# Four whole loads of keys issued as 112, 8 and 8 rows in a decode kernel of two attention layers and two gated feed-forward layers

## The chip, the cores and the metric

The kernel runs on one core of one Trainium2 chip. The metric is the device time in microseconds (us) of one execution. Before the change the median of three runs is 1331.05 us (1328.17, 1331.05 and 1331.53). The profiled execution that all lines below come from took 1329.1 us, of which 1327.3 us lie between its first and its last instruction (the span).

## The reference, cut to what matters

Two sequences (B = 2), one new token each, go through attention, feed-forward, attention and feed-forward; both attention layers read the same cache of 4096 keys and values for 16 heads of 256 numbers, all in float32.

```python
def _A_ref(x, k_cache, v_cache, wq, wo):
    q = (x @ wq).reshape(B, Sq, H, Dh).transpose(0, 2, 1, 3)
    scores = jnp.einsum("bhqd,bhkd->bhqk", q, k_cache) * (Dh ** -0.5)
    p = softmax(scores, axis=-1)
    o = jnp.einsum("bhqk,bhkd->bhqd", p, v_cache)
    return o.transpose(0, 2, 1, 3).reshape(B, Sq, H * Dh) @ wo
def _B_ref(x, W_gate, W_up, W_down):
    gate = x @ W_gate; up = x @ W_up
    return (gate * (gate > 0) * up) @ W_down
x = x + _A_ref(_layernorm(x), A_k_cache, A_v_cache, A_wq, A_wo)
x = x + _B_ref(_layernorm(x), B_W_gate, B_W_up, B_W_down)
x = x + _A_ref(_layernorm(x), A_k_cache, A_v_cache, A_wq, A_wo)
x = x + _B_ref(_layernorm(x), B_W_gate, B_W_up, B_W_down)
```

One layer's keys and values are 2 x 16 x 4096 x 256 numbers each, 268 MB together. They don't fit on the core, so nearly all of them are read twice, once for each attention layer.

## The kernel before, in words

Work goes by *units*. A unit is one head of one sequence, `(h, b)`; there are 32. The first attention pass takes them in the order `first` = (0,0), (0,1), (1,0), ..., (15,1), and the second in the opposite order, so that what the first pass read last can stay on the core for the second. Each unit has 4 MB of keys and 4 MB of values. On the host the keys are laid out so that each of the 128 rows of a unit's keys is one contiguous run of 8192 numbers (32 KB); the same holds for the values. Row p goes to partition p of the core's memory.

The memory for loads is one tile, `arena`: 6 blocks of four slots and 3 single slots, a slot being 8 KB on each partition (1 MB). The class `Arena` hands slots out. A *whole load* (`n == NC`, that is 4) takes a block and brings a unit's 4 MB of keys or of values with one DMA; loads of one slot are used at the ends of the passes, for the head weights (`w_head`, 7 KB a row) and for the feed-forward weights (`w_in`, `w_out`).

`pending` is the list of all loads in the order in which they're to be issued: for each unit its keys, for every second unit the next head's weights, then its values; at the end of a pass the feed-forward weights. `pump` (lines 112 to 134) goes down this list. It takes slots for the first load; if there are none, it stops. If there are, it issues the load on SyncE's queue (SP) at line 132 and goes on. `pump` is called at the start and by `release`, which the compute steps call after the last instruction that reads a slot. So SP's instructions stand in one fixed order: each load waits for the instructions that last read its slots, then it's issued. The loads in flight are as many as the arena has room for.

A load of 128 rows is shared by the core's 16 DMA engines, eight rows each. Only the very last load of the program is cut today: its last 448 columns come as a DMA of their own, in two of 120 and 8 rows (the slices in line 131).

Compute of a unit: `score` (line 332) multiplies the keys by the query on TensorE, one slot at a time, `score_copy` and `score_turn` bring the scores into rows, `softmax_max` and `softmax_exp` use GpSimd and ScalarE, `weigh` (line 392) multiplies by the values, and `project` adds to the output `y`. The order of the instructions on each engine is the program's order (`manual_schedule`); `score` reads columns of a block over all 128 partitions, so it can start when all rows of that unit's load have landed.

In the second pass 22 of the slots hold what the first pass left (`KEPT`), so that the stretch between the passes has few free slots, and the loads there are small.

Of the kernel before, what the change touches and what calls it, by code (L numbers as in the profile page):

```python
# [15 lines left out]
P = 128  # L16
# [5 lines left out]
NC = NT // CT  # L22
# [5 lines left out]
SMALL = 13  # L28
ENDS = 4
AHEAD = 4  # L30
EPS = 1e-5
SCALE = DH**-0.5

# [32 lines left out]
def two_layers(  # L66
# [10 lines left out]
    nc = tc.nc  # L77
# [19 lines left out]
    def source(key, n):  # L97
        kind, name, c = key
        if kind in "kv":
            h, b = name  # L100
            if kind == "k":
                rows = k_cache[b, h]
            else:
                rows = v_cache[b, h].rearrange("(p t) d -> p (t d)", t=NT)
            return rows[:, c * UNIT : (c + n) * UNIT]
        if kind == "h":
            return w_head[name]
        if kind == "in":
            return w_in[c]
        return w_out[:, (14 * c + 2) // 4 * D : (14 * c + 16) // 4 * D]  # L110

    def pump():
        while pending:
            at = None
            for i, ((kind, name, c), n) in enumerate(pending[: AHEAD if pending[0][1] == 1 else 1]):
                if i and kind != "h":
                    continue
                last = at_of.get((kind, name, c - 1)) if kind in "kv" else None
                at = units.take(n, kind, last)
                if at is not None:  # L120
                    break
            if at is None:
                return
            pending.pop(i)
            src = source((kind, name, c), n)
            dst = arena[:, at * UNIT : at * UNIT + src.shape[1]]
            parts = [0, src.shape[1]]
            if not pending:
                parts[1:1] = [src.shape[1] - D]
            for i, j in zip(parts, parts[1:]):  # L130
                for p in (slice(0, 120), slice(120, P)) if i else (slice(0, P),):
                    nc.sync.dma_start(dst[p, i:j], src[p, i:j])
            for k in range(n):
                at_of[kind, name, c + k] = at + k

# [4 lines left out]
    def release(*key):  # L140
        units.free.add(at_of.pop(key))
        pump()
# [42 lines left out]
    found_s = consts.tile([P, 2 * DH], F32, name="found_s")  # L185
    nc.scalar.dma_start(row[:B, :D], x.rearrange("b s d -> (b s) d"))
    pump()


# [19 lines left out]
    eps_t = consts.tile([P, 1], F32, name="eps_t")  # L209
    nc.vector.memset(eps_t, EPS)  # L210

# [434 lines left out]
```

## Time and profile before

| | |
|---|---|
| median of three runs | 1331.05 us |
| profiled execution | 1329.1 us |
| its span | 1327.3 us, 13785 instructions |
| TensorE matmul busy | 953.9 us (72%) |
| VectorE, ScalarE, GpSimd busy | 134.7, 92.1 and 47.7 us |
| read from HBM | 561.52 MB, 423 GB/s over the span |
| whole loads of keys, of values | 59 and 58, of 4096 KB each |

How to read the lines of the profile: PE is TensorE's matmuls and PEld its weight loads, DVE is VectorE, ACT ScalarE, POOL GpSimd, SP SyncE; SPq is SyncE's sequencer, which issues the loads. L132 is line 132 of the kernel before. In a line of a group of instructions stand its line, engine, operation, the tile written and the tiles read and the count, then the busy time in us and the mean length of one in ns, then the idle time of the engine just before them and what ended it. In the table by stretches of time each row holds the stretch, its length, the busy time and the count of each engine, TensorE's granted clock (1.00 is full), the mean busy share of the 16 DMA engines, and the GB/s that they moved; the share may come out a little over 1.00 since a packet's time overlaps the next one's. The "DMA queue" lines give packets, MB and the time of the packets as a share of 16 engines over the whole span; q8 and q14 are the core's own fetches of instructions.

### The profile page before, as it was taken

To read this page: it belongs to the slowest core of one execution; us is meant where nothing else is said; L and a number is where in the kernel's file an instruction comes from. 1 tells how busy PE (TensorE), PEld (TensorE's weight loads), DVE (VectorE), ACT (ScalarE), POOL (GpSimd) and SP (SyncE) were. 2 spreads that over 40 slices of the span, in tenths; PEclk is the share of its full clock that TensorE was granted. 3 is DMA by queue.
4 is the path that set the end of the run, shared out by engine and by line. 5 is a ranking of instruction groups with operands and counts; after the bars stand their busy time and mean duration, and the time that the engine had idled before them with its cause. 6 is when DMAs were issued, how large, how long until landed. Compare 5 with 4: busy or idle time off the path is not lost.

```text
span 1327.3 us, 13785 instructions
## 1 busy us (share of the span) xinstructions
PE 953.9 (72%) x6076; PEld 321.5 (24%) x6076; DVE 134.7 (10%) x457; ACT 92.1 (7%) x280; POOL 47.7 (4%) x134
## 2 busy tenths in 40 slices
PE   4758777866677676687788967666776676766777
PEld 2223123221222221222243322222122121222213
DVE  1100011010110110000101111011011010101100
ACT  1000000000000000000011000000000000000001
POOL 0000000000000000000000000000000000000000
PEclk9786776677777876766798887787778777777779
DMA  9999999999999999999999999999999999999997
GB/s 403 434 427 430 430 427 436 428 433 426 427 436 432 429 430 426 433 433 428 422 370 403 430 430 430 431 430 430 430 429 431 431 432 427 430 434 430 430 422 300
DMA packets 27871, 562.42 MB, mean 424 GB/s; under 512 B 3101, under 2 KB 3235, under 8 KB 10019
## 3 DMA queue, kind: packets, MB, share of 16 engines
q1 hardware_dynamic: 27803, 561.53, 99.0%
q8 instruction: 48, 0.79, 0.2%
q14 instruction: 12, 0.10, 0.0%
q10 hardware_dynamic: 8, 0.01, 0.0%
HBM read 561.52 MB, written 0.00 MB: 423 GB/s over the span
## 4 chain that ended last, share of the span: by engine, by line
PE 61%; another core or an unknown queue 20%; DMA 12%; DVE 3%; issue 2%; ACT 1%; POOL 0%; SPq 0%; POOLq 0%; ACTq 0%; DVEq 0%
PE pob L392 12%; PE rawa L332 12%; PE rawb L332 12%; PE poa L392 11%; PE small L346 5%; PE pq L308 4%; DMA arena<-in_k_cache_dram 4%; DMA arena<-in_v_cache_dram 3%; DMA arena<-in_w_in_dram 3%; PE small L418 3%; DVE found_s L340 3%; DMA arena<-in_w_out_dram 2%; PE pq L311 1%; PE y L248 1%
## 5 line engine op out<-in xcount | busy, mean ns | idle before, releaser
L332 PE MATMUL rawb<-arena,q_pad 128*2 128x512 f32 x1024 | 177.3, 828 | 96.3 <-DMA arena<-in_k_cache_dram 96.3
L332 PE MATMUL rawa<-arena,q_pad 128*2 128x512 f32 x1024 | 176.9, 825 | 92.2 <-DMA arena<-in_k_cache_dram 91.7
L392 PE MATMUL poa<-arena,probs 128*2 128x512 f32 x1024 | 167.7, 815 | 72.7 <-DMA arena<-in_v_cache_dram 46.3
L392 PE MATMUL pob<-arena,probs 128*2 128x512 f32 x960 | 176.6, 902 | 47.0 <-DMA arena<-in_v_cache_dram 47.0
L346 PE MATMUL small<-ident,found_s 128*128 128x8 f32 x512 | 73.3, 270 | 35.5 <-DVE found_s L340 35.4
L346 PEld LDWEIGHTS small<-ident,found_s 128*128 128x128 f32 x512 | 67.4, 205 | 97.9 <-DVE found_s L340 97.9
L392 PEld LDWEIGHTS poa<-arena,probs 128*2 128x2 f32 x1024 | 30.3, 104 | 182.5 <-issue 137.3
L332 PEld LDWEIGHTS rawb<-arena,q_pad 128*2 128x2 f32 x1024 | 24.0, 95 | 191.0 <-DMA arena<-in_k_cache_dram 120.8
L332 PEld LDWEIGHTS rawa<-arena,q_pad 128*2 128x2 f32 x1024 | 24.2, 94 | 187.7 <-issue 172.2
L392 PEld LDWEIGHTS pob<-arena,probs 128*2 128x2 f32 x960 | 29.1, 110 | 166.1 <-issue 166.0
L360 ACT ACTIVATE nm<-top,nsr 128x1 f32<-128x1 f32 x64 | 18.8, 294 | 713.7 <-POOL top L355 713.7
L418 PEld LDWEIGHTS small<-ones,row 128*128 128x128 f32 x256 | 45.7, 253 | 89.9 <-issue 79.1
L355 POOL PARTITION_ALL_REDUCE top<-mx x64 | 22.5, 352 | 1164.7 <-DVE mx L353 1151.3
L308 PE MATMUL pq<-xs,arena 128*128 128x2 f32 x384 | 61.0, 275 | 0.5 <-DVE xs L264 0.5
L308 PEld LDWEIGHTS pq<-xs,arena 128*128 128x128 f32 x384 | 57.6, 225 | 2.0 <-issue 1.3
L418 PE MATMUL small<-ones,row 128*128 128x1 f32 x256 | 51.2, 304 | 2.6 <-DVE row L410 2.2
L427 DVE COPY oT<-small 128x2 f32<-128x2 f32 x64 | 10.2, 159 | 353.0 <-PE small L418 353.0
L410 DVE SCALAR_TENSOR_TENSOR row<-pob,ri,row 128x256 f32<-128x256 f32 x30 | 14.5, 483 | 218.5 <-ACT row L405 218.5
L410 DVE SCALAR_TENSOR_TENSOR row<-poa,ri,row 128x256 f32<-128x256 f32 x32 | 15.5, 483 | 179.6 <-ACT row L405 179.6
L405 ACT ACTIVATE row<-pob,ri 128x256 f32<-128x256 f32 x32 | 15.2, 474 | 254.6 <-PE pob L392 241.6
L340 DVE COPY found_s<-rawb 128x512 f32<-128x512 f32 x32 | 22.1, 691 | 87.5 <-PE rawb L332 87.5
L340 DVE COPY found_s<-rawa 128x512 f32<-128x512 f32 x32 | 22.1, 692 | 76.8 <-PE rawa L332 76.8
(79 smaller groups left out, 310.6 us busy)
## 6 DMA issues: line engine op xcount, KB each, us to landing
arena<-in_k_cache_dram SPq DMA_DIRECT2D x59, 4096.0 KB, 54.9
arena<-in_v_cache_dram SPq DMA_DIRECT2D x58, 4096.0 KB, 55.3
arena<-in_w_head_dram SPq DMA_DIRECT2D x31, 896.0 KB, 54.1
arena<-in_v_cache_dram SPq DMA_DIRECT2D x14, 1024.0 KB, 10.5
arena<-in_w_in_dram SPq DMA_DIRECT2D x14, 896.0 KB, 26.2
arena<-in_k_cache_dram SPq DMA_DIRECT2D x8, 1024.0 KB, 13.2
arena<-in_w_out_dram SPq DMA_DIRECT2D x4, 896.0 KB, 17.4
arena<-in_w_out_dram SPq DMA_DIRECT2D x3, 672.0 KB, 11.9
```

Of the source, the lines that this page charges most:

```text
L248: nc.tensor.matmul(y[at : at + B, : w_h.shape[1]], stat, w_h, **flags)
L308: nc.tensor.matmul(pq[:, j, :], w[:, at : at + P], xT[:, c, :], start=(c == 0), stop=False)
L311: nc.tensor.matmul(pq[:, j, :], w[:, FULL * DH : FULL * DH + P], xT[:, FULL + j, :], start=False, stop=True,)
L332: nc.tensor.matmul(raw[u % 2][32 * g : 32 * g + 2, :], q_of[u][:, j, 1 - half : 3 - half], kt[:, g, :], start=(c == 0), stop=(c == NC - 1),)
L340: nc.vector.tensor_copy(found_s, raw[u % 2])
L346: nc.tensor.matmul(s[:, :, e, :], found_s[:, e * P : (e + 1) * P], pick, start=True, stop=True,)
L355: nc.gpsimd.partition_all_reduce(mx_of[u], mx, P, RED.max)
L360: nc.scalar.activation(nm, mx_of.pop(u), AF.Copy, scale=nsr[:, b : b + 1])
L392: nc.tensor.matmul(po_of[u][32 * t : 32 * t + 2, :], p_of[u][:, n : n + 2], vt[:, 2 * t * DH : (2 * t + 2) * DH], start=(c == 0), stop=(c ...
L405: nc.scalar.activation(row[:, :DH], po_of[u][:, :DH], AF.Copy, scale=r_of[u][:, 0:1])
L410: nc.vector.scalar_tensor_tensor(row[:, :DH], po_of.pop(u)[:, DH:], r_of[u][:, 1:2], row[:, :DH], op0=ALU.mult, op1=ALU.add,)
L418: nc.tensor.matmul(pT_of[u][:, c : c + 1], row[:, c * P : (c + 1) * P], ones, start=True, stop=True,)
```

## The change

A new constant names two units. Where `pump` issues a whole load of keys of one of them, it now issues three DMAs in place of one: rows 0 to 111, rows 112 to 119, and rows 120 to 127. The values of these units, and all other loads, stay as they are. Each unit is loaded once in each pass, so there are four such loads: in the first pass the units at places 10 and 20 of 32, in the second those at places 11 and 21. The bytes, the slots and the order of the loads are the same. A DMA of 112 rows gives each of the 16 engines seven rows; a DMA of eight rows goes to eight engines, one row each. Line 131's cut of the program's last load is dropped by the same edit: `rows` is (0, 128) for it, so that its last 448 columns come as one DMA of 128 rows.

```diff
 AHEAD = 4
+UNEVEN = ((5, 0), (10, 0))
 EPS = 1e-5
@@ in pump()
             for i, j in zip(parts, parts[1:]):
-                for p in (slice(0, 120), slice(120, P)) if i else (slice(0, P),):
-                    nc.sync.dma_start(dst[p, i:j], src[p, i:j])
+                rows = (0, 112, 120, P) if n == NC and name in UNEVEN and kind == "k" else (0, P)
+                for p, r in zip(rows, rows[1:]):
+                    nc.sync.dma_start(dst[p:r, i:j], src[p:r, i:j])
             for k in range(n):
                 at_of[kind, name, c + k] = at + k
```

## The prediction

> **What bounds the kernel now.** I read the page first: the DMA rows, then the groups of TensorE.
>
> ```profile
> span 1327.3 us, 13785 instructions
> DMA  9999999999999999999999999999999999999997
> q1 hardware_dynamic: 27803, 561.53, 99.0%
> q8 instruction: 48, 0.79, 0.2%
> L332 PE MATMUL rawb<-arena,q_pad 128*2 128x512 f32 x1024 | 177.3, 828 | 96.3 <-DMA arena<-in_k_cache_dram 96.3
> L332 PE MATMUL rawa<-arena,q_pad 128*2 128x512 f32 x1024 | 176.9, 825 | 92.2 <-DMA arena<-in_k_cache_dram 91.7
> arena<-in_k_cache_dram SPq DMA_DIRECT2D x59, 4096.0 KB, 54.9
> arena<-in_w_out_dram SPq DMA_DIRECT2D x1, 210.0 KB, 14.6
> ```
>
> SP's queue has the DMA engines at work for 99.0% of the span, and TensorE's idle time before the scores ends with a load of keys. So the loads bound the kernel, and a load is issued 54.9 us before it lands: many are queued on each DMA engine. Next, the stretches: a steady one, then the ends of both passes cut fine.
>
> ```profile
> core 0: us, PE busy (x) PEld busy (x) DVE busy (x) ACT busy (x) POOL busy (x), PEclk, DMA share, GB/s
> 30.00:640.00 610.00, 442.58 (x2640) 148.11 (x2640) 59.90 (x196) 37.13 (x120) 22.06 (x60) 0.72 1.00 430
> ...
> 666.00:668.00 2.00, 2.00 (x22) 0.71 (x20) 0.00 (x0) 0.23 (x1) 0.00 (x0) 1.00 0.97 401
> 668.00:670.00 2.00, 1.57 (x15) 0.88 (x15) 0.16 (x1) 0.41 (x2) 0.00 (x0) 1.00 0.74 308
> 670.00:672.00 2.00, 1.73 (x15) 1.19 (x17) 0.33 (x2) 0.31 (x2) 0.00 (x0) 1.00 0.49 195
> 672.00:674.00 2.00, 2.00 (x24) 0.67 (x24) 0.18 (x2) 0.00 (x0) 0.00 (x0) 1.00 0.36 57
> ```
>
> ```profile
> 1314.00:1315.00 1.00, 0.80 (x9) 0.26 (x10) 0.00 (x0) 0.00 (x0) 0.00 (x0) 1.00 0.98 396
> 1315.00:1316.00 1.00, 0.57 (x6) 0.10 (x2) 0.62 (x1) 0.00 (x0) 0.00 (x0) 1.00 0.89 330
> 1316.00:1317.00 1.00, 1.00 (x11) 0.96 (x12) 0.00 (x0) 0.00 (x0) 0.00 (x0) 1.00 0.66 231
> 1317.00:1318.00 1.00, 1.00 (x19) 0.60 (x18) 0.18 (x1) 0.00 (x0) 0.00 (x0) 1.00 0.54 220
> 1318.00:1319.00 1.00, 1.00 (x18) 0.52 (x13) 0.00 (x0) 0.00 (x0) 0.00 (x0) 1.00 0.50 203
> 1319.00:1320.00 1.00, 1.00 (x8) 0.26 (x3) 0.00 (x0) 0.00 (x0) 0.00 (x0) 1.00 0.49 190
> 1320.00:1321.00 1.00, 0.37 (x9) 0.17 (x12) 0.00 (x0) 0.00 (x0) 0.00 (x0) 1.00 0.21 57
> 1321.00:1322.00 1.00, 0.80 (x16) 0.27 (x8) 0.00 (x0) 0.07 (x1) 0.00 (x0) 1.00 0.05 20
> ```
>
> In the steady stretch all 16 engines are busy and move 430 GB/s, 26.9 each. At the end the share doesn't fall at once: it drops to about a half by 1317, stays at 0.50 and 0.49 until 1320, and then goes to nothing. Half of the engines run dry early. With x the share, the late half works (4 x 0.5 + 0.49 + 0.21 + 0.05) / 0.5 = 5.5 us past 1315, the early half the other 0.39 + 0.16 + 0.04, over 0.5, or 1.2 us: **4.3 us** apart. At the end of the first pass the same stair stands at 0.74, 0.49 and 0.36. The instruction queue q8 offers a reason: 0.2% of 16 engines over 1327.3 us is 42 us (32 to 53 with the rounding), 21 in each pass; on half of the engines it is 2.7 us each. Which engines these are, no row says.
>
> **The change part by part.**
>
> *The rows moved.* A whole load is 4096 KB, or 4.194 MB; at 430 GB/s it takes 9.75 us, and one 32 KB row takes its engine an eighth, 1.22 us. Nine rows in place of eight cost the first eight engines 1.22 us in each such load; seven save the others as much. Two loads a pass make plus and minus 2.44 us, 4.88 us between the halves, about the 4.3 us read above. If each row costs what it costs now, and the late half is just the last eight, a pass ends up to 2.44 us earlier.
>
> *How the rows travel.* The trace before has no 32 KB rows in a DMA of eight rows. Its only narrow pieces, 120 and 8 rows of the last load, are the very end of the table. The bounds: at least 1.22 us for such a DMA (each engine writes its row at its usual speed), at most 9.75 us (the eight go one behind another, like the eight rows of one engine today). The nearest row is 1320 to 1321, when little but the last pieces is left: 0.21 of 16 engines is 3.4 busy engines, and they move 57 GB/s, 17.0 each and not 26.9. The second before, with wider loads in it, has 190 / (0.49 x 16) = 24.2. Busy engines that move 0.63 of their usual bytes look like engines that wait for one another at the place they write to. I take those 57 GB/s as what a narrow piece gets: 8 x 32,768 B / 57 GB/s = **4.6 us**, between the bounds. It's the weakest step here, since these rows were only 1792 B long and short rows alone could cost speed.
>
> [...]
>
> *The sum for one such load on the first eight engines*: seven rows at 1.22 are 8.5 us, two narrow pieces 9.2, together 17.7 in place of 9.75, so **+8.0 us**. What follows on these engines is queued behind, and as the engines are busy all the time, nothing is caught up within the pass: +16.0 us for two. The piece of 112 rows may itself lie between 8.5 us and the full load's 9.75, as its seven rows an engine no longer fall on the same places as eight; I take half, 0.6 a load, 1.2 a pass. That makes 17.2.
>
> *What of it shows.* The first eight engines may end a pass early today; between 0 us (they're as late as the others) and 4.3 of it is hidden. As no row tells which half is which, I take 3, nearer the upper end, since only a half that is all of one kind gives so clean a stair: 17.2 - 3 = 14.2 us a pass. Each pass's end follows its slowest engine: the last product waits for the last piece of `w_out`, and the stretch before 674 has the engines idle until the first pass's compute frees slots.
>
> ```profile
> 1303.31 17.41 DMA arena<-in_w_out_dram
> 1320.76 0.53 PEld L248 LDWEIGHTS y<-arena,near 128*2 128x2 f32 x16 [1.13 <-DMA arena<-in_w_out_dram]
> L132 SPq DMA_DIRECT2D arena<-in_k_cache_dram x67: 327/328/811, 1.2 to 1224.2; - x67
> ```
>
> *SP.* Eight DMAs more, 328 ns each, 2.6 us in all. They're hidden by the 54.9 us for which loads are queued ahead; without that cover they'd cost the 2.6. Behind the three issues of a load only the next loads wait. The wait for a slot isn't new, but TensorE now waits for three landings and not one, the last of which is late by the sum above; it then has 54.9 us of work queued less some 17 of lag, so the engines that are ahead don't run dry. Lost cover there would show as a share under 1.00 inside a pass.
>
> *The last load.* It comes as 128 rows again: eight engines lose one 1792 B row and the sixteenth engine gets eight. At 26.9 GB/s that is 0.07 and 0.53 us; if the sixteenth is among the early ones it's nothing, if it's the last, 0.5 later; one narrow piece less may give 0.2 back. I take 0.
>
> *The sum*: 1329.1 + 2 x 14.2 = 1357.5 us for the profiled execution. The median of the runs shown is 1331.05, 1.95 higher, so **1359.5 us** for the median of after.
>
> **The rivals.**
>
> *The balance works* (faster). Narrow pieces run at 1.22 us and the late half is the last eight: the late engines end 2.44 us earlier, the early ones later by 2.44 and just meet them. 1331.05 - 2 x 2.44 = 1326.2. For it: the stair's 4.3 us against the 4.88 of the change. Against: the 57 GB/s, and that the late engines needn't be the last eight.
>
> *The wrong engines* (no gain, though pieces run at full speed). If the late ones stand on both sides, some of the first eight are late and get 2.44 more a pass, at most 4.9 in all; where they're a little less late than the latest it's about 1. 1331 to 1336, I say 1332. The trace doesn't speak against it.
>
> *Full speed nearly* (a little slower). Each engine of a narrow piece keeps the 17.0 GB/s that it had at 1320, since their rows don't all collide: 32,768 / 17.0 is 1.93 us a piece. A load costs 8.5 + 3.9 - 9.75 = 2.7, a pass 5.4 - 3 = 2.4: 1335.9.
>
> *The neighbours join in* (much slower). The other engines go on with the next load and write the last rows too, so that ten rows and not eight share the 57 GB/s: 5.7 us a piece, a load 8.5 + 11.5 - 9.75 = 10.2, a pass 20.5 + 1.2 - 3 = 18.7: 1368.4. With lag growing through the second load it could reach 25 a pass, 1381.
>
> *The cut isn't what it says.* If a DMA of eight rows isn't spread over eight engines but goes through one, a piece takes 9.75 us on that one engine: 8.5 + 19.5 - 9.75 = 18.3 a load, 36.5 - 3 a pass: 1398. The program's last load, cut in that way, landed 14.6 us after its issue among others that did so too, which speaks against a special path but doesn't tell how many engines took part.
>
> [...]
>
> **How the numbers follow.** Forecast 0.38, neighbours 0.19, one engine 0.03, nearly full speed 0.10, wrong engines 0.18, balance 0.12. Predicted is 1359.5. A measurement of this kernel can tell about 0.3%, 4 us, from no change. Faster by more: the balance, 0.12, of which 0.02 stays inside: 0.10. Within: those 0.02, most of the wrong engines (0.17) and 0.05 of the nearly full speed: 0.24. Slower: 0.66. For 8 in 10 the range leaves out the balance's 0.10, the serial case and the far end of the neighbours: 1329 to 1384. The forecast's own range, with narrow pieces between 3.5 and 5.7 us and 0 to 4.3 hidden, is 1346 to 1374.
>
> **What would show it.** If I'm right, the whole loads of keys that are cut land later, TensorE's idle time before line 332 grows by some 8 us at four places, the share stays near 1.00 until the pass's end, and then the stair at about half is three or four times as long as now. The narrow pieces, 256 KB each, stand in the list of issues. If the balance works, the stair is gone: the share falls from 0.9 to nothing within two us, and the span is 4 to 5 us shorter. If the stair is as long as now with the same span, the wrong engines were relieved. I'm wrong at the first step if the DMA share falls inside a pass, and at the narrow pieces if the time is below 1340.

## The result and the profile after

The change makes the kernel **slower by 5.7%**: 1405.09 us (1403.47 to 1407.99) against 1330.22 us for the kernel before, ratio 1.0572 with a 95% interval of 1.056 to 1.0585. That is 74.9 us, or 18.7 us for each of the four loads that are cut. The direction was forecast, the size was not: 1359.5 us were predicted, and 1405 lies above the range. The profiled execution took 1403.47 us.

The page of the profile after, in the order of the lines shown of before (the edit moves the later lines down by two, so that 332 is now 334; the row of GB/s is the span in 40 equal slices):

```profile
span 1401.7 us, 13801 instructions
DMA  9999999999999999999989999999999999999996
GB/s 399 440 430 431 430 429 238 429 430 429 431 426 274 365 429 430 432 429 429 420 334 411 430 429 430 368 316 430 429 430 433 419 213 429 434 431 432 429 422 252
q1 hardware_dynamic: 27860, 561.53, 98.6%
L334 PE MATMUL rawb<-arena,q_pad 128*2 128x512 f32 x1024 | 197.1, 911 | 133.3 <-DMA arena<-in_k_cache_dram 133.3
L334 PE MATMUL rawa<-arena,q_pad 128*2 128x512 f32 x1024 | 171.2, 801 | 126.7 <-DMA arena<-in_k_cache_dram 125.0
arena<-in_k_cache_dram SPq DMA_DIRECT2D x4, 3584.0 KB, 70.4
```

The DMA engines are as busy as before and the bytes are the same; what fell is what busy engines move. Four dips stand in the row of GB/s, each at one of the cut loads: 238, 274 with 365, 368 with 316, and 213. TensorE's idle time before the scores that ends with a load of keys grew from 188.0 to 258.3 us, 70.3 of the 74.9. That is no exact account, since TensorE's waits for values fell from 93.3 to 79.9 us, and its busy time grew from 953.9 to 972.7 us at a mean granted clock of 0.735 in place of 0.762; the bytes that the engines moved, further down, are the firmer count. Where the wait for keys falls is shown by the longest single waits (us in total, times, longest), before (L332) and after (L334):

```profile
PE rawb L332 <- DMA arena<-in_k_cache_dram: 96.3, 27, 4.5
PE rawa L332 <- DMA arena<-in_k_cache_dram: 91.7, 28, 4.6
PE rawb L334 <- DMA arena<-in_k_cache_dram: 133.3, 27, 19.7
PE rawa L334 <- DMA arena<-in_k_cache_dram: 125.0, 26, 19.3
```

Cut finer around the first of these loads, after the kernel's own columns of stretches (engines' busy time, granted clock, DMA share, GB/s):

```profile
190.00:210.00 20.00, 14.99 (x72) 3.55 (x72) 1.33 (x3) 0.47 (x1) 0.00 (x0) 0.59 1.04 433
210.00:226.00 16.00, 10.64 (x54) 5.39 (x53) 1.14 (x5) 1.24 (x4) 0.73 (x2) 0.61 1.00 234
226.00:238.00 12.00, 0.00 (x0) 0.00 (x0) 0.00 (x0) 0.00 (x0) 0.00 (x0) 0.50 0.96 131
238.00:258.00 20.00, 12.83 (x84) 3.52 (x84) 1.92 (x6) 1.24 (x4) 0.73 (x2) 0.76 0.98 415
```

Two steps. For 16 us the engines move 234 GB/s, which is 3.74 MB, about the piece of 112 rows (3.67 MB). Then come 12 us at 131 GB/s, and the two narrow pieces must lie there: TensorE has nothing left to do, as it waits for them. Against 430 GB/s the first step loses 16 x (1 - 234/430) = 7.3 us, the second 12 x (1 - 131/430) = 8.3 us.

Which engines are slow can be read from the trace's own records of packets, most of which are one row of 32 KB. From 206 to 245 us 15 to 17 of them are in flight at every moment, so all 16 engines are at work throughout. (The DMA share counts a packet where it starts; that is why a short stretch can show 0.96 or 1.04.) Before 208 us a row takes 1.22 us in the median. Rows that start from 212 to 224 take 1.75 to 2.60 us, and rows that start from 228 to 234.5 take 4.08 to 4.74 us. None is fast. How a DMA's rows are shared shows in the packets too. They stand in 16 series at a time, in each of which a row starts a few ns from another's end, and I read a series as one engine. In the profile before, eight rows of a whole load come between two packets of 4 B (707 times from 100 to 600 us, where series can be followed). In this first cut load it's seven, and then a packet of 4 B stands behind each single row of the narrow pieces: 32 such packets start from 222 to 239, and 16 + 8 + 8 are 32. In five series two such single rows stand one behind the other. The counts of packets under 512 B say the same of the experiments below: four more DMAs of 64 rows are 64 more packets (`r64`, 3165 against 3101), 16 more of eight rows are 128 (`r96_c8`, 3229). In this first load 30 rows took over 4.0 us, and the two pieces have only 16 rows: the engines without a narrow piece are as slow as those with one.

The same reckoning over the four dips, after one row of before for comparison:

```profile
200.00:260.00 60.00, 48.91 (x260) 18.98 (x264) 5.41 (x19) 3.24 (x11) 2.20 (x6) 0.61 1.01 434
```

```profile
200.00:260.00 60.00, 33.32 (x184) 11.69 (x188) 3.91 (x13) 2.48 (x8) 1.47 (x4) 0.61 1.01 319
400.00:480.00 80.00, 42.27 (x260) 12.63 (x260) 5.77 (x19) 3.24 (x11) 2.20 (x6) 0.68 1.00 330
890.00:960.00 70.00, 39.38 (x236) 12.62 (x240) 5.79 (x19) 3.45 (x12) 2.20 (x6) 0.71 1.01 343
1110.00:1170.00 60.00, 28.21 (x144) 10.62 (x144) 3.31 (x10) 2.00 (x7) 1.47 (x4) 0.62 1.00 298
```

The losses are 15.5, 18.6, 14.2 and 18.4 us, 66.7 in all, so nine tenths of the change's cost lie in these four stretches. In this profile the second cut load of each pass costs more than the first.

The end of the program:

```profile
1382.00:1384.00 2.00, 1.94 (x24) 0.47 (x16) 0.00 (x0) 1.63 (x2) 0.00 (x0) 1.00 1.02 409
1384.00:1386.00 2.00, 1.64 (x17) 0.54 (x13) 0.49 (x3) 0.46 (x2) 0.00 (x0) 1.00 0.89 366
1386.00:1388.00 2.00, 1.22 (x14) 0.33 (x10) 0.00 (x0) 0.00 (x0) 0.00 (x0) 1.00 0.59 237
1388.00:1390.00 2.00, 1.57 (x15) 0.65 (x7) 0.62 (x1) 0.00 (x0) 0.00 (x0) 1.00 0.21 84
1390.00:1391.00 1.00, 1.00 (x13) 0.68 (x16) 0.19 (x1) 0.00 (x0) 0.00 (x0) 0.75 0.12 50
...
1392.00:1393.00 1.00, 1.00 (x7) 0.26 (x2) 0.00 (x0) 0.00 (x0) 0.00 (x0) 0.50 0.13 54
...
1394.00:1395.00 1.00, 1.00 (x20) 0.40 (x15) 0.00 (x0) 0.00 (x0) 0.00 (x0) 1.00 0.05 18
```

The stair at one half, which stood from 1317 to 1320 before, is gone. The share falls to 0.21 by 1388, and then a tail goes on to 1396 in which about two of the 16 engines work (0.12 x 16). By the same reckoning the stretch from 1384 to 1396 loses 8.3 us, where the end before, from 1314 to 1322, lost 4.2; the end of the first pass loses 1.0 us more than before. So half of the engines did not carry the extra time to the end of the pass, as the prediction had it: 66.7 us are lost by all 16 where the cut loads are, and some 5 us more where a few engines end a pass late.

### The profile page after: what moved, and what is told of

It reads as the page before. It is cut to its first block, busy times and chain, and to the rows that moved or that the text cites. A ratio compares the mean times of both kernels' runs of the same rounds, so it can differ in the third digit from the quotient of the medians.

```text
span 1401.7 us, 13801 instructions
## 1 busy us (share of the span) xinstructions
PE 972.7 (69%) x6076; PEld 327.9 (23%) x6076; DVE 134.8 (10%) x457; ACT 92.1 (7%) x280; POOL 47.7 (3%) x134
## 3 DMA queue, kind: packets, MB, share of 16 engines
q1 hardware_dynamic: 27860, 561.53, 98.6%
## 4 chain that ended last, share of the span: by engine, by line
PE 59%; another core or an unknown queue 22%; DMA 12%; DVE 3%; issue 2%; ACT 1%; POOL 0%; SPq 0%; POOLq 0%; ACTq 0%; DVEq 0%
PE rawb L334 12%; PE rawa L334 11%; PE poa L394 11%; PE pob L394 10%; DMA arena<-in_k_cache_dram 7%; PE small L348 5%; DMA arena<-in_v_cache_dram 3%; PE pq L310 3%; PE small L420 3%; DVE found_s L342 2%; DMA arena<-in_w_in_dram 2%; PE pq L313 1%; PE y L250 1%; DMA arena<-in_w_out_dram 0%
## 5 line engine op out<-in xcount | busy, mean ns | idle before, releaser
L334 PE MATMUL rawb<-arena,q_pad 128*2 128x512 f32 x1024 | 197.1, 911 | 133.3 <-DMA arena<-in_k_cache_dram 133.3
L334 PE MATMUL rawa<-arena,q_pad 128*2 128x512 f32 x1024 | 171.2, 801 | 126.7 <-DMA arena<-in_k_cache_dram 125.0
L394 PE MATMUL poa<-arena,probs 128*2 128x512 f32 x1024 | 174.1, 843 | 73.3 <-DMA arena<-in_v_cache_dram 49.9
L394 PE MATMUL pob<-arena,probs 128*2 128x512 f32 x960 | 169.0, 868 | 30.0 <-DMA arena<-in_v_cache_dram 30.0
L334 PEld LDWEIGHTS rawb<-arena,q_pad 128*2 128x2 f32 x1024 | 25.1, 99 | 239.2 <-DMA arena<-in_k_cache_dram 139.5
L394 PEld LDWEIGHTS poa<-arena,probs 128*2 128x2 f32 x1024 | 31.5, 106 | 188.0 <-issue 140.3
L334 PEld LDWEIGHTS rawa<-arena,q_pad 128*2 128x2 f32 x1024 | 24.4, 94 | 217.6 <-issue 202.6
L412 DVE SCALAR_TENSOR_TENSOR row<-poa,ri,row 128x256 f32<-128x256 f32 x32 | 15.5, 484 | 186.6 <-ACT row L407 186.6
```

Source lines behind the costliest of these rows:

```text
L334: nc.tensor.matmul(raw[u % 2][32 * g : 32 * g + 2, :], q_of[u][:, j, 1 - half : 3 - half], kt[:, g, :], start=(c == 0), stop=(c == NC - 1),)
L394: nc.tensor.matmul(po_of[u][32 * t : 32 * t + 2, :], p_of[u][:, n : n + 2], vt[:, 2 * t * DH : (2 * t + 2) * DH], start=(c == 0), stop=(c ...
L412: nc.vector.scalar_tensor_tensor(row[:, :DH], po_of.pop(u)[:, DH:], r_of[u][:, 1:2], row[:, :DH], op0=ALU.mult, op1=ALU.add,)
```

## The experiments

All kernels below are the kernel before, with one or more whole loads of keys cut in another way; the cut of the program's last load stays as it was (but in `ctl_cut`). The common edit, and then only its third line, which says which rows and columns each DMA takes:

```diff
+UNEVEN = ((5, 0), (10, 0))
+    def cuts_of(n, kind, name, i, j):
+        if n == NC and name in UNEVEN and kind == "k":
+            return [(p, 0, NC * UNIT) for p in (...)]
+        rows = (slice(0, 120), slice(120, P)) if i else (slice(0, P),)
+        return [(p, i, j) for p in rows]
-                for p in (slice(0, 120), slice(120, P)) if i else (slice(0, P),):
-                    nc.sync.dma_start(dst[p, i:j], src[p, i:j])
+                for p, a, b in cuts_of(n, kind, name, i, j):
+                    nc.sync.dma_start(dst[p, a:b], src[p, a:b])
```

My theory after the result: the rows of a short piece go to few places of the memory, and the engines that write there share what the places take (A). The rivals: each DMA more has its price (B), or the unequal shares themselves cost the time (C).

**Number of DMAs: `cols3`.**

```diff
+            return [(slice(0, P), a, b) for a, b in ((0, 7168), (7168, 7680), (7680, 8192))]
```

> The four whole loads of keys come as three DMAs each, as in the change, but cut by columns: 128 rows with 7168, 512 and 512 of the 8192 columns. Theory A (the places in memory that the rows of a short piece go to limit it): no change against before, 1330 us within 0.3%, since every DMA still goes to all 128 rows. Rival B (each further DMA, its issue and its landing cost the time): eight more DMAs as in the change, so the change's 75 us, 1405 us. Rival C (nine rows on one half of the engines and seven on the other): no change, each engine has eight rows.

Measured: 1329.41 against 1328.74 us, ratio 1.001 (1.0001 to 1.0019). Eight DMAs more, cut by columns, cost at most 0.2%. B falls.

**Halves: `r64`.**

```diff
+            return [(p, 0, NC * UNIT) for p in (slice(0, 64), slice(64, 128))]
```

> The four whole loads of keys come as two DMAs each, rows 0 to 63 and rows 64 to 127, every engine four rows of each. [...] Rival B (number of DMAs): one more DMA a load and not two, half of the change's 75 us, 1367 us; the run with cuts by columns tells it from A. Rival C (unequal engines): no change, 1330 us.

Measured: 1382.75 us, ratio 1.0407 (1.0391 to 1.0422), +54.0 us or 13.5 a load. All engines have equal shares here, and it still costs nearly three quarters of the change. C falls as the main cause. The stretch of the slow load, in `r64`:

```profile
190.00:210.00 20.00, 14.14 (x82) 4.26 (x82) 1.92 (x6) 0.70 (x3) 0.43 (x2) 0.74 1.02 428
210.00:232.00 22.00, 6.64 (x45) 2.17 (x44) 1.04 (x4) 1.24 (x4) 0.69 (x2) 0.69 1.01 203
```

About half of the speed, 203 of 430 GB/s, but for longer than one load: 13.5 us are lost and not the 9.75 of a load at half speed. The packets show that all engines are alike here too: every row of 32 KB that starts from 212 to 226 takes 2.33 to 2.72 us, against 1.22. In the four dips 139 to 174 rows take over 1.5 us, where the load has 128, so rows of the neighbouring loads are slow as well; that adds to the 9.75.

**Equal shares with the change's first piece: `r112_16`.**

```diff
+            return [(p, 0, NC * UNIT) for p in (slice(0, 112), slice(112, 128))]
```

> The four whole loads of keys come as 112 and 16 rows, so that every one of the 16 engines carries seven rows and one: the change's first piece, without its unequal shares. Theory A (places): the piece of 112 rows moves 238 GB/s as in the profile of after, 15.4 us for 3.67 MB and not 8.5, and 16 neighbouring rows are as slow as eight and eight were, 115 GB/s, 4.6 us and not 1.2: +10.3 us a load, +41 us, 1371 us. Rival C (unequal engines): no change, 1330 us. Rival B: one more DMA a load, 1367 us.

Measured: 1384.73 us, ratio 1.0418 (1.04 to 1.0435), +14.0 us a load where A said 10.3. Without any unequal share, three quarters of the change's price are there. The first of these loads in `r112_16`:

```profile
210.00:222.00 12.00, 10.57 (x54) 5.40 (x53) 1.13 (x5) 1.24 (x4) 0.73 (x2) 0.60 0.98 242
222.00:234.00 12.00, 0.00 (x0) 0.00 (x0) 0.00 (x0) 0.00 (x0) 0.00 (x0) 0.54 0.99 178
```

So 112 rows are as slow here, at 242 GB/s, as in the change, with no piece of eight rows behind them.

**The rest of the edit: `ctl_cut`.**

```diff
-        rows = (slice(0, 120), slice(120, P)) if i else (slice(0, P),)
+            return [(slice(0, P), i, j)]
+        rows = (slice(0, P),) if i else (slice(0, P),)
```

> Only the other part of the edit: the program's last 448 columns come as one DMA of 128 rows in place of 120 and 8. All theories: no change, 1330 us within 2 us, as the prediction took 0 for it; if the cut was worth something, up to 1 us longer.

Measured: 1328.58 us, ratio 0.9997 (0.9988 to 1.0006). The cut of the last 448 columns is worth nothing that can be measured.

**Bytes or a fixed price: `eighth`.**

```diff
+            return [(slice(0, P), 0, 7168)] + [(p, 7168, 8192) for p in (slice(0, 112), slice(112, 120), slice(120, P))]
```

> The four loads come as 128 rows for 7168 of the 8192 columns, and the cut into 112, 8 and 8 rows is made in the last 1024 columns only. Theory A (bandwidth of the places): the loss goes by the bytes in the short pieces, an eighth of 75 us, +9 us, 1339 us. Rival B' (a fixed price of a short or unequal DMA, whatever its bytes): the change's 75 us, 1404 us.

Measured: 1338.93 against 1329.46 us, ratio 1.007 (1.0054 to 1.0087): +9.5 us, where an eighth of 74.9 is 9.4. The price goes by the bytes that are cut into 112, 8 and 8 rows. Rows of 4 KB cost the same per byte here as rows of 32 KB.

**Where the rows go: `r96_c8` and `r96_s8`.** Same engines, bytes and number of DMAs; only the rows of the four pieces differ.

```diff
+            return [(p, 0, NC * UNIT) for p in (slice(0, 96), slice(96, 104), slice(104, 112), slice(112, 120), slice(120, 128))]
```

> One of a matched pair. The four whole loads of keys come as rows 0 to 95 (six rows an engine) and then four DMAs of eight neighbouring rows, 96 to 103, 104 to 111, 112 to 119, 120 to 127. Theory A (places): 96 rows at the 2.2 us a row of the change's first piece are 13.2 us, four narrow pieces at 4.6 us are 18.4, together 31.6 us in place of 9.75: +22 us a load, +87 us, 1416 us. Rival C (unequal engines: ten rows on eight engines, six on the others): 2 rows more, 2.4 us a load, at most +10 us, and the same as its twin.

```diff
+            return [(p, 0, NC * UNIT) for p in (slice(0, 96), slice(96, 128, 4), slice(97, 128, 4), slice(98, 128, 4), slice(99, 128, 4))]
```

> The twin: the same DMAs on the same engines with the same bytes, but each of the four DMAs of eight rows takes every fourth row, 96, 100, ..., 124, then 97, 101, ..., 125, and so on. [...] Rival C (unequal engines): the same as its twin. Rival D (a DMA of eight rows is slow wherever its rows go): the same as its twin.

Measured: 1437.8 us with neighbouring rows, ratio 1.0821 (1.0797 to 1.0846), and 1409.42 us with every fourth row, 1.0596 (1.0578 to 1.0613). The twins differ by 28.4 us, 7.1 a load: C and D fall as stated, since both say the same for both. But the neighbouring pieces are dearer than A's sum of 1416 us, and the spread ones aren't cheap either: which rows are taken makes 28.4 of the 108.3 us that the neighbouring pieces cost; the spread ones still cost 80.0. The stretches of the neighbouring pieces, in `r96_c8`:

```profile
210.00:224.00 14.00, 8.10 (x53) 3.17 (x52) 1.23 (x5) 1.24 (x4) 0.73 (x2) 0.71 1.03 224
224.00:244.00 20.00, 0.00 (x0) 0.00 (x0) 0.00 (x0) 0.00 (x0) 0.00 (x0) 0.50 1.00 134
```

and of the strided ones, in `r96_s8`:

```profile
210.00:224.00 14.00, 5.97 (x32) 1.00 (x32) 0.48 (x1) 0.47 (x1) 0.00 (x0) 0.62 1.02 225
224.00:238.00 14.00, 0.00 (x0) 0.00 (x0) 0.00 (x0) 0.00 (x0) 0.00 (x0) 0.50 0.99 201
```

The 96 rows run at 224 and 225 GB/s in both. The pieces then take all 16 engines to 134 GB/s where rows are neighbours and to 201, about half of 430, where they're spread. In both the DMA share stays at 1.00 and 0.99: the eight engines without a piece are busy and slow too. The packets say the same: rows that start from 229 to 236 take 2.45 to 2.55 us in `r96_s8`, those from 229 to 240 take 3.78 to 4.24 us in `r96_c8`, and none takes 1.22.

**Every second row: `r64s2`.**

```diff
+            return [(p, 0, NC * UNIT) for p in (slice(0, 128, 2), slice(1, 128, 2))]
```

> [...]

The two DMAs of 64 rows of `r64`, but the even and the odd rows in place of the halves. Measured: 1329.43 against 1328.96 us, ratio 1.0007 (0.9997 to 1.0017): no price at all, where the same two DMAs with the halves cost 54 us. The stretch in which `r64` had 203 GB/s, here:

```profile
210.00:232.00 22.00, 16.73 (x110) 8.01 (x114) 2.57 (x10) 2.00 (x7) 1.47 (x4) 0.73 1.01 434
```

So two DMAs of 64 rows aren't slow as such: neighbours run at 203 GB/s, every second row at 434. But neighbouring rows alone aren't it either: 128 of them run at 430 GB/s, and 112, seven eighths, at 234. One statement could cover both, engines that meet at one place share it and a DMA's shape decides whether they meet; it is argued, not shown: no run tells which rows share a place. Nor do these runs tell the writing from the reading: each cut changes the rows that are read from HBM together with the partitions that are written, so a cause on the reading side stands untested.

**The pieces on the other side: `r96_e8` and `r96_ec8`.** First rows 32 to 127, then pieces in rows 0 to 31, every fourth row in the one and neighbours in the other.

```diff
+            return [(p, 0, NC * UNIT) for p in (slice(32, 128), slice(0, 32, 4), slice(1, 32, 4), slice(2, 32, 4), slice(3, 32, 4))]
```

> As the run with 96 rows and four strided pieces of eight, mirrored: first rows 32 to 127, then rows 0, 4, ..., 28, then 1, 5, ..., 29, and so on. [...] Rival D' (a strided or narrow piece costs what it cost in the run before, 1409 us, wherever it goes): 1409 us.

```diff
+            return [(p, 0, NC * UNIT) for p in (slice(32, 128), slice(0, 8), slice(8, 16), slice(16, 24), slice(24, 32))]
```

> As the run with rows 32 to 127 first and strided pieces in rows 0 to 31, but the four pieces are neighbouring rows: 0 to 7, 8 to 15, 16 to 23, 24 to 31. [...] If a blocked engine also holds up engines that write elsewhere, all 16 fall to one speed and the total is about the 128 GB/s of the run with neighbouring pieces in rows 96 to 127. [...]

Measured: `r96_e8` 1384.65 us, ratio 1.043 (1.0407 to 1.0452), 24.8 us shorter than the strided pieces in rows 96 to 127, so D' falls. `r96_ec8` 1410.68 us, ratio 1.0619 (1.0599 to 1.0638), 26.0 us longer than `r96_e8`. The stretches of `r96_e8`:

```profile
210.00:224.00 14.00, 9.55 (x51) 4.87 (x51) 1.14 (x5) 1.23 (x4) 0.73 (x2) 0.68 1.03 226
224.00:229.00 5.00, 0.00 (x0) 0.00 (x0) 0.00 (x0) 0.00 (x0) 0.00 (x0) 0.68 0.92 236
229.00:249.00 20.00, 13.39 (x72) 3.73 (x76) 1.43 (x5) 0.76 (x3) 0.73 (x2) 0.59 1.00 429
```

and of `r96_ec8`:

```profile
224.00:242.00 18.00, 0.00 (x0) 0.00 (x0) 0.00 (x0) 0.00 (x0) 0.00 (x0) 0.55 0.97 180
```

Spread over rows 0 to 31, the pieces are through 5 us after the 96 rows; spread over rows 96 to 127, it took 14. So the place matters, and not the stride by itself. With neighbours in rows 0 to 31 the total is 180 GB/s, and not the 134 of `r96_c8`. The packets again show no engine at full speed: no row of 32 KB that starts from 225 to 239 takes less than 2.34 us, where an undisturbed one takes 1.22. So the slowness reaches engines without a piece here too, at a higher common speed than I had; how, these runs don't say.

**One unit at a time: `one` and `other`.**

```diff
+UNEVEN = ((5, 0),)
```

> The change for one of the two units only, (5, 0), once in each pass. Theory A: each such load costs the same by itself, so half of the change's 75 us: 1367 us. If the first such load of a pass is partly hidden by the early engines, as the prediction had it, the saving is uneven: less than half is left, below 1362.

```diff
+UNEVEN = ((10, 0),)
```

> The change for the other unit only, (10, 0), once in each pass. The change costs 75 us and (5, 0) alone 33. If each load costs by itself and the two units differ: 75 - 33 = 42 us, 1371 us. If a pass hides part of one load but not of a second one: the same 33 us as with (5, 0) alone, 1362 us.

Measured: 1362.06 us, ratio 1.0245 (1.0218 to 1.0272), and 1365.83 us, 1.0281 (1.0247 to 1.0314): +32.6 and +36.9 us, with intervals of 29 to 36 and 33 to 42 us, which overlap. The first lies at the border of its two cases, the second between its two values, so neither decides. Together they make 69.5, a little less than the change's 74.9, but the 5.4 us of difference lie within the intervals. That the second load of a pass costs more, by 3 to 4 us, stands only in the four dips of the one profile read above; its cause is open.

**The balance without blocks of rows: `clean10_6` against `r32s4`.** Every second row across all 128 is free (ratio 1.0007), and so is every fourth (1.0009, the control below), so a load can be cut without the 112 rows. The control keeps eight rows on each engine:

```diff
+UNEVEN = ((10, 0),)
+            return [(p, 0, NC * UNIT) for p in (slice(0, 128, 2), slice(1, 128, 4), slice(3, 128, 4))]
```

> Control for the run with ten and six rows: the whole load of keys of unit (10, 0), once in each pass, comes as rows 0, 2, 4, ... (64 rows), then 1, 5, 9, ... and 3, 7, 11, ... (32 rows each), every engine eight rows in all. If every second row was free because each engine still kept to its own places, every fourth row is free too: no change, 1329 us within 2 us. If 32 rows meet as 64 neighbouring ones did (+13.5 us a load for the whole of it), half of each such load is slow: +13 us, 1342 us.

```diff
+UNEVEN = ((10, 0),)
+            return [(p, 0, NC * UNIT) for p in (slice(0, 128, 2), slice(1, 128, 4), slice(3, 32, 4), slice(35, 64, 4), slice(67, 96, 4), slice(99, 128, 4))]
```

> What the change was to do, with pieces that meet as little as can be: the same load of (10, 0), once in each pass; of the control's last 32 rows each eight go in a DMA of their own: 3, 7, ..., 31, then 35, ..., 63, then 67, ..., 95, then 99, ..., 127. The first eight engines carry ten rows and the others six: in one load what the change moves in two. Balance theory (engines set the end of a pass, and the late half is the last eight): up to 2.4 us a pass shorter than the control, 4.9 us in all, 1324 us, if the pieces are free. [...]

Measured, beside 1328.15 us of before: the control 1329.27 us, ratio 1.0009 (1.0 to 1.0017); ten and six rows 1341.35 us, 1.0095 (1.0081 to 1.0109). The version with unequal shares is 12.1 us slower than its control, 6.0 a load. What they do to the end of the program stands in these two tables, the control first:

```profile
1319.00:1320.00 1.00, 0.64 (x6) 0.67 (x6) 0.21 (x1) 0.00 (x0) 0.00 (x0) 1.00 0.70 235
1320.00:1321.00 1.00, 1.00 (x16) 0.67 (x19) 0.19 (x1) 0.00 (x0) 0.00 (x0) 1.00 0.61 244
1321.00:1322.00 1.00, 1.00 (x24) 0.56 (x14) 0.00 (x0) 0.00 (x0) 0.00 (x0) 1.00 0.52 208
1322.00:1323.00 1.00, 1.00 (x12) 0.43 (x7) 0.00 (x0) 0.00 (x0) 0.00 (x0) 1.00 0.45 181
1323.00:1324.00 1.00, 0.53 (x7) 0.03 (x8) 0.00 (x0) 0.00 (x0) 0.00 (x0) 1.00 0.40 134
```

and with ten and six rows:

```profile
424.00:434.00 10.00, 0.90 (x12) 0.00 (x0) 0.48 (x1) 0.47 (x1) 0.00 (x0) 0.66 1.03 262
...
1325.00:1326.00 1.00, 0.21 (x5) 0.16 (x8) 0.00 (x0) 0.00 (x0) 0.00 (x0) 1.00 0.90 375
1326.00:1327.00 1.00, 1.00 (x10) 0.17 (x2) 0.15 (x1) 0.00 (x0) 0.00 (x0) 1.00 0.85 326
1327.00:1328.00 1.00, 0.57 (x5) 0.41 (x4) 0.47 (x1) 0.00 (x0) 0.00 (x0) 1.00 0.78 314
1328.00:1329.00 1.00, 1.00 (x9) 0.72 (x9) 0.19 (x1) 0.00 (x0) 0.00 (x0) 0.68 0.56 176
1329.00:1330.00 1.00, 1.00 (x15) 0.56 (x15) 0.00 (x0) 0.00 (x0) 0.00 (x0) 0.50 0.31 115
1330.00:1331.00 1.00, 1.00 (x11) 0.29 (x3) 0.00 (x0) 0.00 (x0) 0.00 (x0) 0.50 0.14 52
```

The stair near a half turns into one near 0.9, from which the share falls to 0.14; then it stays at 0.12 and 0.13 to 1333, which is about two engines. Most engines now end nearly together, but the end as a whole isn't more even, by one profile of each: against 430 GB/s it loses 6.8 us from 1323 to 1335, where the control loses 4.8 from 1318 to 1326. The pieces cost more than that: 10 us at 262 GB/s in the first such load and 10 us at 253 in the second lose 8.0 us together. What evening out would be worth if the pieces were free stays open: no cut was found that gives unequal shares at full speed.

## Why the prediction was wrong, step by step

*What bounds the kernel*: right. SP's queue still has the DMA engines at work for 98.6% of the span, and nine tenths of the loss are bytes that these busy engines didn't move while the cut loads came in.

*The narrow pieces*: the size was close. Taken were 4.6 us for a piece and 9.2 us for the two of a load; the rows in that stretch take 4.08 to 4.74 us each, and the stretch lasts 12 us. That is luck in part, since the 57 GB/s behind it came from rows of 1792 B at the very end, with 3.4 engines busy. That it matters which rows a piece takes was shown by the twins (28.4 us), and that the price goes by the bytes by the cut in an eighth of the columns (9.5 us). The mechanism, engines that wait for one another at the place they write to, covers a part at most: engines without a piece are as slow, and whether writing is what they wait for is open.

*The piece of 112 rows*: **this step failed**. It was taken as at most as slow as a full load, 8.5 to 9.75 us with 0.6 of loss; that its rows fall on other places than those of a full load was my estimate, and no run shows where rows fall. The stretch has 234 GB/s for 16 us, a loss of 7.3 us a load, and `r112_16` has 242 GB/s. The upper bound was no bound: I let a DMA of fewer rows cost no more than one of 128, as if 16 engines with seven rows each wrote as freely as with eight. `r64` shows that equal shares on 16 engines can run at half speed, 203 GB/s. Why seven neighbouring rows an engine are slow and eight aren't stays open.

*What of it shows*: **failed too**. The prediction charged the first eight engines alone and let 3 us a pass disappear in their being early. All 16 engines slow down, with 16 packets in flight and 131 GB/s, and the stair at a half was gone at the end and not three or four times as long. No hidden part shows: the ends of the two passes lose some 5 us more than before, and not less. This is the rival of the neighbours, and it went further than its 1381: that rival let only the two rows of the usual writers join.

The sum, measured in place of forecast: 7.3 + 8.3 is 15.6 us for the first cut load where 8.0 + 0.6, less the hidden 1.5, was forecast; the second loads add about 3 to 4 us each in this profile, and the ends of the passes some 5 us in all.

*SP*: right. Cut by columns, as many DMAs cost 0.2% at most. *The last load*: right, ratio 0.9997. *The balance*: its chance of 0.12 was for pieces at full speed, which there were none of; `clean10_6` shows that unequal shares take away the stair at a half, but leave about two engines late, so that the end loses more and not less.

The signs named in advance came out mixed: TensorE's idle time grew by 17.6 us and not by 8 at four places, the share stayed near 1.00, and the stair did the opposite of what was said: it went, and a tail of about two engines came in its place.

No version here beats the kernel before.

## What to carry to other kernels

Don't split a load by blocks of rows to shift work between DMA engines without measuring it: in this kernel blocks of 112, 96 and 64 neighbouring rows ran at 234, 225 and 203 GB/s, about half of the 430 of 128 rows, with equal shares too (`r112_16` 242, `r64` 203). If a load has to be cut, try columns first, or every second or fourth row across all 128: each was free here (ratios 1.001, 1.0007 and 1.0009), while every fourth row within a block of 32 was not (201 GB/s in rows 96 to 127, 236 in rows 0 to 31). And when a DMA share stays at 1.00 while the GB/s fall, as to 234 and 131 here, look first at which rows each DMA takes, not at how many DMAs or bytes there are.

## What the runs showed of the hardware

Unexpected were three things. Loads of 112, 96 and 64 neighbouring rows moved 234, 225 and 203 GB/s on 16 busy engines that move 430 with 128 rows. The same two DMAs of 64 rows moved 434 with every second row. And while eight engines had pieces of eight neighbouring rows, all 16 were busy and moved 131 to 134 GB/s together, so that engines which had no such piece were slow as well; with those pieces in rows 0 to 31 it was 180. In all these stretches the rows in flight at one time slow down together: 1.22 us a row at full speed, 1.75 to 2.60 us during the 112 rows of the change's first cut load, 4.08 to 4.74 us during its pieces of eight.
